# Expert tiles of routed batches written between the transforms of later batches, with transforms of 39 by 64

## The chip, the cores and the metric

The kernel runs on one core of a Trainium2 chip. Its time is the device time of one execution in microseconds (us), the median of several; a profile of one execution shows every instruction of the engines: TensorE (PE, with its weight loads as PEld), VectorE (DVE), ScalarE (ACT), GpSimd (POOL) and SyncE (SP, which here issues transfers). Everything is computed in f32.

## The reference

Eight sequences of 2496 tokens with 256 channels are filtered in the frequency domain; then each token goes to the one of eight experts with the largest logit.

```
X = rfft(x, axis=1); Y = X * (filt_r + 1j * filt_i); y = irfft(Y, n=2496)    # x: 8, 2496, 256
t = y.reshape(19968, 256)
logits = t @ w_gate;  e = argmax(logits);  p = exp(logits - max) / (sum + 1e-9) at e
out = p * (relu(t @ w1[e]) @ w2[e])            # w1: 8, 256, 1024; w2: 8, 1024, 256
```

## The kernel before

A sequence of 2496 is split in 96 and 26, and its transform runs in four products with tables of sines and cosines. A (`stage_a`, L251 on) transforms over the 96 in 26 columns, two to a product of 512 columns, and stores z to DRAM. B and C (`stage_bc`) load z the other way round: B transforms over the 26 for one frequency class a product (256 columns), VectorE multiplies two classes by the filter in one operation of 104 x 1024 (L275), and C transforms back (L282, L286) and stores u. D (`stage_d`) loads u, transforms back over the 96 (L301), stores the tokens to `yd` in DRAM, turns them (L307) and takes the logits (L315). A strip is four columns or four classes, one load and one store each.

`route` finds each token's expert on VectorE, counts tokens per expert with two small products (L351, L352), and GpSimd scatters each token's number and gate into a table in DRAM that is sorted by expert, one indirect transfer a column (L373, 26 a batch).

The batches run in rounds: B and C of batch b, A of batch b + 1 and D of batch b - 1 are handed out strip by strip in turn (`run_all`). A scheduler orders the instructions of this part on each engine. When all eight are routed, `tile_map` makes a list of expert tiles on VectorE: 31 tiles of 512 rows, 8 of 256 and 23 of 128, each of one expert. All of w2 (8 MB) is loaded then and stays on the chip; w1 of a tile's expert (1 MB) is loaded tile by tile.

The expert part is in the order it is written in. For a tile: `gather` loads its part of the table and gathers its rows, 128 at a time, on GpSimd's queue (L490); `turn_x` turns them on PE (L506); `hidden` makes eight products over the 256 channels with relu (L517, halves of 128); `result` sums over the 1024 hidden values for each 128 rows (L531), scales by the gate and scatters the rows to the output on GpSimd's queue (L537). PE's order is hidden of tile i, turn of tile i + 1, result of tile i - 1.

In the profile, each f32 product stands as two records on PE (L531 x2608 are 1304 products), a turn as one.

Of the kernel before, what the change touches and what calls it, by code (L numbers as in the profile page):

```python
# [25 lines left out]
N1 = 96  # L26
N2 = 26
G = N2 // 2
NP = N1 // 4
K2 = 4 * N2  # L30
# [4 lines left out]
def dft_tables():  # L35

    q = np.arange(N1)
    t = np.arange(N2)
    g = np.arange(G)
    w = 2.0 * np.pi

    ta = np.zeros((N1, 2, 2, NP))
    td = np.zeros((2, 2, NP, N2, N1))
    n = N2 * q[None, :] + t[:, None]
    for s in range(2 * NP):  # L50
        h, p = divmod(s, NP)
        if s == 0:
            ta[:, h, 0, p] = 1.0
            ta[:, h, 1, p] = (-1.0) ** q
            td[h, 0, p] = 1.0
            td[h, 1, p] = (-1.0) ** q[None, :]
        else:
            ang = w * ((q * s) % N1) / N1
            ta[:, h, 0, p] = np.cos(ang)
            ta[:, h, 1, p] = -np.sin(ang)  # L60
            ang = w * ((n * s) % S) / S
            td[h, 0, p] = np.cos(ang)
            td[h, 1, p] = -np.sin(ang)
    td *= 2.0 / S


    tb = np.zeros((N2, 2, 2, NP, 2, 2, 2, G))
    for s in range(2 * NP):
        h, p = divmod(s, NP)
        for u in range(2):  # L70
            k = ((N1 - s if s else N1 // 2) if u else s) + N1 * g
            ang = w * ((t[:, None] * k[None, :]) % S) / S
            c, sn = np.cos(ang), np.sin(ang)
            if s == 0:
                tb[:, h, u, p, 0, h, u] = c
                tb[:, h, u, p, 1, h, u] = -sn
            else:
                i = -1.0 if u else 1.0
                tb[:, h, 0, p, 0, h, u] = c
                tb[:, h, 1, p, 0, h, u] = i * sn  # L80
                tb[:, h, 0, p, 1, h, u] = -sn
                tb[:, h, 1, p, 1, h, u] = i * c
    tb[:, 0, :, 0, 1, 0, 0, 0] = 0.0
    tb[:, 0, 0, 0, 1, 0, 0, 0] = (-1.0) ** t


    y = np.zeros((2, 2, 2, 2, G, N2, 2, 2))
    for z in range(2):
        for h in range(2):
            for u in range(2):  # L90
                if z and h == 0:
                    k = (N1 // 2 if u else 0) + N1 * g
                    ang = w * ((k[:, None] * t[None, :]) % S) / S
                    y[z, 0, h, u, :, :, h, u] = np.cos(ang)
                    y[z, 1, h, u, :, :, h, u] = -np.sin(ang)
                    if u == 0:
                        y[z, 0, h, u, 0, :, h, u] = 0.5
                        y[z, 1, h, u, 0, :, h, u] = 0.5 * (-1.0) ** t
                else:
                    ang = w * (((g[:, None] + u) * t[None, :]) % N2) / N2  # L100
                    i = -1.0 if u else 1.0
                    y[z, 0, h, u, :, :, h, 0] = np.cos(ang)
                    y[z, 1, h, u, :, :, h, 0] = -np.sin(ang)
                    y[z, 0, h, u, :, :, h, 1] = i * np.sin(ang)
                    y[z, 1, h, u, :, :, h, 1] = i * np.cos(ang)

    yq = np.stack([y[:, 1], -y[:, 0]], axis=1)
    yq[1, :, 0, 0, 0] = 0.0
    tc = np.stack([y, yq], axis=1).reshape(4, K2, K2).transpose(1, 0, 2)

    return {
        "ta": ta.reshape(N1, N1),
        "tb": tb.reshape(K2, NP, K2),
        "tc": tc,
        "td": td.reshape(N1, N2, N1),
    }
# [3 lines left out]
def kernel(  # L120
# [3 lines left out]
    filt_r: bass.AP,  # L124
    filt_i: bass.AP,
# [6 lines left out]
    td: bass.AP,  # L132
    out: bass.AP,
# [3 lines left out]
    B = x.shape[0]  # L137
    N = B * S

    TILES, left = [], N  # L140
    for rows in (512, 256):
        n = (left - E * (rows - 1)) // rows
        TILES.append((rows, n))
        left -= rows * n
    TILES.append((P, (left + E * (P - 1)) // P))
    TR = E * N + (E + 1) * P
    TR = (TR + 4 * P - 1) // (4 * P) * (4 * P)

    dram = ctx.enter_context(tc.tile_pool(name="dram", bufs=1, space=DRAM))
    zd = [dram.tile([N2, 4, NP, D], F32, tag=f"z{b % 2}", name="zd") for b in range(B)]  # L150
    ud = [dram.tile([N2, 4, NP, D], F32, tag=f"u{b % 2}", name="ud") for b in range(B)]
# [6 lines left out]
    cnt = perm.tile([N1, E], F32, name="cnt")  # L158
    em8 = perm.tile([N1, E], F32, name="em8")
    eoff = perm.tile([N1, E], F32, name="eoff")  # L160
# [4 lines left out]
    psb = fft.enter_context(tc.tile_pool(name="psb", bufs=5, space=PSUM))  # L165
    pst = fft.enter_context(tc.tile_pool(name="pst", bufs=2, space=PSUM))
    psr = fft.enter_context(tc.tile_pool(name="psr", bufs=1, space=PSUM))

    tas = cst.tile([N1, N1], F32, name="tas")
    tbs = cst.tile([K2, NP, K2], F32, name="tbs")  # L170
    tcs = cst.tile([K2, 4, K2], F32, name="tcs")
    tds = cst.tile([N1, N2, N1], F32, name="tds")
    ht = cst.tile([K2, 2, NP, D], F32, name="ht")
    wg = cst.tile([P, DH, E], F32, name="wg")
    tri = cst.tile([N1, N1], F32, name="tri")
    ones = cst.tile([N1, N1], F32, name="ones")
    seg = cst.tile([N1, E, N2], F32, name="seg")
    fill = cst.tile([P, 64, 2], I32, name="fill")
    zrow = cst.tile([1, D], F32, name="zrow")
    ids0 = cst.tile([N1, N2], I32, name="ids0")  # L180
    e_i = cst.tile([N1, E], I32, name="e_i")

    def bank():
        return psb.tile([P, 512], F32, tag="bank", name="bank")

    turn = [0]

    def evac(o, i):
        turn[0] += 1
        if turn[0] % 2:  # L190
            nc.scalar.copy(out=o, in_=i)  # L191
        else:
            nc.vector.tensor_copy(o, i)

    xv = x.rearrange("b (q t) d -> b q t d", t=N2)
    CH = [(t0, min(4, N2 - t0)) for t0 in range(0, N2, 4)]
    PH = [(p0, 4) for p0 in range(0, NP, 4)]


    nc.sync.dma_start(out=tas, in_=ta)  # L200

    def load_filters():
        nc.sync.dma_start(out=tbs, in_=tb)
        for s, f in enumerate((filt_r, filt_i)):
            for h in range(2):
                r = 26 * h
                nc.sync.dma_start(
                    out=ht[r:r + G, s],
                    in_=bass.AP(f.tensor, f.offset + NP * h * D, [[N1 * D, G], [D, NP], [1, D]]),
                )  # L210
                p0 = 1 - h
                nc.sync.dma_start(
                    out=ht[r + G:r + 2 * G, s, p0:],
                    in_=bass.AP(f.tensor, f.offset + (N1 - NP * h - p0) * D, [[N1 * D, G], [-D, NP - p0], [1, D]]),
                )
            nc.sync.dma_start(
                out=ht[G:2 * G, s, 0:1],
                in_=bass.AP(f.tensor, f.offset + N1 // 2 * D, [[N1 * D, G], [D, 1], [1, D]]),
            )
            nc.sync.dma_start(out=ht[2 * N2:K2, s], in_=ht[0:2 * N2, s])  # L220
            nc.sync.dma_start(out=ht[2 * N2:2 * N2 + 1, s, 0, :], in_=f[S // 2:S // 2 + 1, :])
        nc.sync.dma_start(out=tcs, in_=tcm)
# [3 lines left out]
    make_identity(nc, ident)  # L226
    nc.gpsimd.memset(ones, 1.0)
    nc.gpsimd.affine_select(
        out=tri, in_=ones, compare_op=ALU.is_gt, fill=0.0, base=0, pattern=[[1, N1]], channel_multiplier=-1
    )  # L230
    nc.gpsimd.memset(seg, 1.0)
    nc.gpsimd.memset(seg[:, :, 0:1], 0.0)
    nc.gpsimd.memset(cnt, 0.0)
    nc.gpsimd.memset(fill[:, :, 0:1], N)
    nc.gpsimd.memset(fill[:, :, 1:2], 0)
    nc.gpsimd.iota(ids0, pattern=[[1, N2]], base=0, channel_multiplier=N2)
    nc.gpsimd.iota(e_i, pattern=[[1, E]], base=0, channel_multiplier=0)
    nc.vector.tensor_scalar(em8, in0=e_i, scalar1=-float(E), scalar2=None, op0=ALU.add)
    nc.vector.tensor_scalar(eoff, in0=e_i, scalar1=float(N), scalar2=None, op0=ALU.mult)

    def fill_table():
# [6 lines left out]
        nc.sync.dma_start(out=yd[N:N + 1, :], in_=zrow)  # L248


    def stage_a(b):  # L251
        for t0, n in CH:
            xt = sb.tile([N1, 4, D], F32, tag="in", name="xt", bufs=7)
            nc.sync.dma_start(out=xt[:, :n], in_=xv[b, :, t0:t0 + n, :])
            zo = sb.tile([N1, 4, D], F32, tag="st", name="zo", bufs=5)
            for j in range(0, n, 2):
# [329 lines left out]
```

## Time and profile before

| | |
|---|---|
| median of 3 runs | 2347.44 us (2342.65 to 2349.18) |
| the profiled execution | 2343.8 us, span 2342.1 us |
| PE busy | 1904.0 us, 81% of the span |
| mean granted clock of TensorE | 0.873 |
| POOL, DVE, ACT busy | 512.7, 465.6, 323.7 us |
| moved by DMA | 248.33 MB, mean 106 GB/s |

The span runs from the first to the last instruction. A granted clock of 1.00 is 2.4 GHz, 0.50 is 1.2 GHz; a mean between them says what part of a stretch stood at which. Busy time of PE is the time in which a product is in the array, so at a low clock the same work is more busy time. A row of the timeline merges like instructions: start, length, engine, line, operation, and in brackets how long the engine had been idle and what ended it.

### The profile page before, as it was taken

To read this page: it belongs to the slowest core of one execution; us is meant where nothing else is said; L and a number is where in the kernel's file an instruction comes from. 1 tells how busy PE (TensorE), PEld (TensorE's weight loads), DVE (VectorE), ACT (ScalarE), POOL (GpSimd) and SP (SyncE) were. 2 spreads that over 40 slices of the span, in tenths; PEclk is the share of its full clock that TensorE was granted. 3 is DMA by queue.
4 is the path that set the end of the run, shared out by engine and by line. 5 is a ranking of instruction groups with operands and counts; after the bars stand their busy time and mean duration, and the time that the engine had idled before them with its cause. 6 is when DMAs were issued, how large, how long until landed. Compare 5 with 4: busy or idle time off the path is not lost. (4 is left out here: it accounts for less than half of the span.)

```text
span 2342.1 us, 22213 instructions
## 1 busy us (share of the span) xinstructions
PE 1904.0 (81%) x7622; PEld 1261.6 (54%) x7622; DVE 465.6 (20%) x862; ACT 323.7 (14%) x652; POOL 512.7 (22%) x552
## 2 busy tenths in 40 slices
PE   0568858585858677574389999999999999999998
PEld 0224434342434334353156666666666666788997
DVE  0122313131223213122011111111111111111221
ACT  0111111120111111110011111111111111111221
POOL 0000120304040301223332222222222222232221
PEclk9888777786769668675689999999999999999999
DMA  7745434444454535131532222222222221223552
GB/s 143 190 132 155 121 106 129 98 144 90 127 118 145 118 97 153 54 106 27 180 137 85 76 75 72 75 72 75 72 75 75 75 76 65 81 95 117 160 177 74
DMA packets 127203, 248.33 MB, mean 106 GB/s; under 512 B 28007, under 2 KB 79923, under 8 KB 126740
## 3 DMA queue, kind: packets, MB, share of 16 engines
q1 hardware_dynamic: 104792, 204.90, 30.7%
q0 software_dynamic: 22304, 42.01, 5.9%
q8 instruction: 66, 1.08, 0.2%
q14 instruction: 41, 0.34, 0.1%
HBM read 161.05 MB, written 84.16 MB: 105 GB/s over the span
## 5 line engine op out<-in xcount | busy, mean ns | idle before, releaser
L517 PE MATMUL hps<-xT,w1t 128*128 128x512 f32 (+2 forms) x1984 | 577.3, 449 | 0.0
L531 PE MATMUL yps<-w2s,hT 128*128 x2608 | 574.0, 379 | 0.0
L531 PEld LDWEIGHTS yps<-w2s,hT 128*128 128x128 f32 x2608 | 490.7, 190 | 64.9 <-issue 0.3
L517 PEld LDWEIGHTS hps<-xT,w1t 128*128 128x128 f32 x1984 | 324.2, 191 | 234.8 <-issue 224.7
L373 POOL DMA_INDIRECT table<-pay,row x208 | 190.4, 915 | 908.5 <-DVE row L370 569.2
L537 POOL DMA_INDIRECT out_dram<-ys,idt x163 | 163.0, 1000 | 796.4 <-DVE ys L535 540.3
L286 PE MATMUL bank<-pq,tcs 104*104 104x512 f32 x352 | 232.9, 797 | 108.4 <-DVE pq L275 104.5
L520 DVE TENSOR_SCALAR hT<-hps 128x512 f32<-128x512 f32 (+2 forms) x248 | 126.2, 509 | 551.9 <-PE hps L517 539.4
L315 PE MATMUL lg<-wg,yt 128*96 128x8 f32 x832 | 97.8, 244 | 128.3 <-ACT yt L191 62.7
L275 DVE TENSOR_TENSOR pq<-bank,ht 104x1024 f32<-104x1024 f32 x96 | 117.5, 1224 | 364.4 <-PE bank L271 295.8
L521 ACT ACTIVATE hT<-hps 128x512 f32<-128x512 f32 (+2 forms) x248 | 111.9, 451 | 489.4 <-PE hps L517 444.9
L286 PEld LDWEIGHTS bank<-pq,tcs 104*104 104x104 f32 x352 | 66.2, 211 | 203.9 <-DVE pq L275 131.7
L490 POOL DMA_INDIRECT xg<-yd,idt x163 | 157.2, 964 | 83.2 <-issue 45.8
L315 PEld LDWEIGHTS lg<-wg,yt 128*96 128x96 f32 x832 | 94.7, 189 | 147.9 <-ACT yt L191 70.7
L258 PE MATMUL bank<-xt,tas 96*96 96x512 f32 x208 | 119.2, 705 | 65.5 <-DMA xt<-in_x_dram 65.5
L271 PE MATMUL bank<-zi,tbs 104*104 104x256 f32 x384 | 134.6, 476 | 18.1 <-DMA zi<-zd 18.1
L287 ACT COPY uo<-bank 104x512 f32<-104x512 f32 x96 | 56.3, 586 | 575.4 <-PE bank L286 453.2
L271 PEld LDWEIGHTS bank<-zi,tbs 104*104 104x104 f32 x384 | 79.6, 220 | 73.8 <-issue 56.8
L258 PEld LDWEIGHTS bank<-xt,tas 96*96 96x96 f32 x208 | 40.3, 197 | 135.5 <-issue 65.9
L535 DVE TENSOR_SCALAR ys<-yps,idt 128x256 f32<-128x256 f32 x82 | 39.6, 483 | 364.3 <-PE yps L531 364.3
L301 PE MATMUL bank<-ui,tds 96*96 96x256 f32 x416 | 110.3, 404 | 2.0 <-DMA ui<-ud 2.0
L536 ACT ACTIVATE ys<-yps,idt 128x256 f32<-128x256 f32 x81 | 38.4, 474 | 486.6 <-PE yps L531 486.6
(83 smaller groups left out, 648.1 us busy)
## 6 DMA issues: line engine op xcount, KB each, us to landing
w1t<-in_moe_w_dram SPq DMA_DIRECT2D x62, 1024.0 KB
zi<-zd SPq DMA_DIRECT2D x48, 416.0 KB
ud<-uo SPq DMA_DIRECT2D x48, 416.0 KB
xt<-in_x_dram SPq DMA_DIRECT2D x48, 384.0 KB
zd<-zo SPq DMA_DIRECT2D x48, 384.0 KB
ui<-ud SPq DMA_DIRECT2D x48, 384.0 KB
yd<-yo SPq DMA_DIRECT2D x48, 384.0 KB
w2s<-in_moe_w_dram SPq DMA_DIRECT2D x8, 1024.0 KB
```

What stands on the lines that cost most here:

```text
L258: mm(ps[:N1, :], lhsT=tas, rhs=xt[:, j:j + 2, :], start=True, stop=True)
L271: mm(ps[:K2, i * D:(i + 1) * D], lhsT=tbs[:, p0 + j + i, :], rhs=zi[:, j + i, :], start=True, stop=True)
L275: nc.vector.tensor_mul(pq, z2[:, None].to_broadcast((K2, 2, 2, D)), ht[:, :, p0 + j:p0 + j + 2, :])
L286: mm(ps[:K2, :], lhsT=tcs[:, s, :], rhs=pq[:, s], start=(s == 0), stop=(s == 1))
L315: mm(lg[:, 0, t * E:(t + 1) * E], lhsT=yt[:, 2 * i + dh, :], rhs=wg[:, dh, :], start=(dh == 0), stop=(dh == DH - 1))
L373: sc = nc.gpsimd.indirect_dma_start(out=table, out_offset=bass.IndirectOffsetOnAxis(ap=row[:, t:t + 1], axis=0), in_=pay[:, t, :], in_offs ...
L490: nc.gpsimd.indirect_dma_start(out=xgs[i][:, j], out_offset=None, in_=yd, in_offset=bass.IndirectOffsetOnAxis(ap=idt[i].bitcast(U32)[:, j, ...
L517: mm(ps[:, :m], lhsT=w1[:, dh, k * P:(k + 1) * P], rhs=xT[:, dh, :m], start=(dh == 0), stop=(dh == DH - 1))
L520: either(lambda: nc.vector.tensor_scalar_max(hT[:, :m], ps[:, :m], 0.0), lambda: nc.scalar.activation(hT[:, :m], ps[:, :m], AF.Relu))
L521: lambda: nc.scalar.activation(hT[:, :m], ps[:, :m], AF.Relu))
L531: mm(ps, lhsT=hT[k][:, j * P:(j + 1) * P], rhs=w2s[:, bass.ds(ev, 1), k, :], start=(k == 0), stop=(k == FT - 1))
L537: nc.gpsimd.indirect_dma_start(out=out, out_offset=bass.IndirectOffsetOnAxis(ap=ids.bitcast(U32)[:, j, 0:1], axis=0), in_=ys, in_offset=No ...
```

## The change

The sequence is split in 39 and 64. Since three blocks of 39 fill 117 rows, one matrix carries three columns at once: columns 0 to 21, 22 to 42 and 43 to 63 stand in three blocks of partitions (`T0`, `NB`), so there are 22 columns of 117 rows instead of 26 of 96. The 39 real values of a column are 20 frequency classes, so B and C have 20 classes instead of 24, with 128 rows (two halves of 64, real and imaginary) instead of 104. x and the filters are laid out on the host in the order in which they are loaded.

The filter multiply is three multiplies of 512 columns on VectorE and an add on GpSimd for each pair of classes. z and u are stored and loaded in three pieces (one for each block of 39) or two (for each half of 64).

Tiles are made batch by batch: `GROUPS` gives for each batch how many tiles of 512 rows are sure to be full by then (0, 1, 5, 5, 5, 5, 5, 5; the 8 of 256 and 23 of 128 follow the last). w2 is loaded tile by tile as w1 is, two buffers each, and all of it only for the tiles of 128 rows. `transform` and `experts` are two lists of steps with a planned cost each, and one loop writes them out: a tile's step goes next when its inputs should have landed by the planned clock and the credit isn't used up, else a transform step; a transform step gives 2.7 times its cost as credit. PE, VectorE, ScalarE and SP run in the order thus written; GpSimd's order is left to the scheduler. D of a batch is written behind C of the same batch, and A of the next batch between B and C; C of a strip follows B of the next. Copies out of PSUM go to VectorE or ScalarE by planned load, and all stages share seven banks of PSUM.

```diff
-N1 = 96
-N2 = 26
+N1 = 39
+N2 = 64
+NF = (N1 + 1) // 2
+T0 = (0, 22, 43)
+NB = len(T0)
+NG = 22
+TP = NB * N1
...
+    for b in range(B):
+        n = max(0, ((b + 1) * S - (N - left) - E * 511) // 512)
+        GROUPS.append([(512, n)])
+        left -= 512 * n
...
+    def stage_b(b, c):
...
+            for i in range(2):
+                k = HP if f + i == 0 else P
+                mm(p[:, i * D:(i + 1) * D], lhsT=tbs[:k, f + i, :], rhs=zi[:k, j + i, :], start=True, stop=True)
...
+            nc.vector.tensor_mul(yv, z2, ht[:, 0, f:f + 2, :])
+            nc.vector.tensor_mul(yw[:HP], z2[HP:], ht[:HP, 1, f:f + 2, :])
+            nc.vector.tensor_mul(yw[HP:], z2[:HP], ht[HP:, 1, f:f + 2, :])
+            free["v"] = max(free["v"], now[0]) + 2.1
+            ys = outs["y", b, f] = sb.tile([P, 2, D], F32, tag="ysum", name="ysum", bufs=3)
+            nc.gpsimd.tensor_tensor(ys, yv, yw, op=ALU.add)
...
+    def weights(i, second):
...
+        if second:
+            w2t[i] = moe.tile([P, FT, D], F32, tag="w2t", name="w2t")
+            nc.sync.dma_start(out=w2t[i], in_=moe_w2[bass.ds(ev, 1)].rearrange("o p i d -> p (o i) d"))
...
+    def transform():
...
+        for b in range(B):
+            for i in range(nb + 1):
+                if i < nb:
+                    yield lambda: stage_b(b, i), 1.7, None
+                if b + 1 < B:
+                    yield lambda: stage_a(b + 1, i), 0.43 * CH[i][1], ("a", b + 1) if i == nch - 1 else None
+                if 1 <= i:
+                    yield lambda: stage_c(b, i - 1), 1.7, ("c", b) if i == nb else None
+            for i in range(nch + 2):
+                if i < nch:
+                    yield lambda: stage_d(b, i), 0.43 * CH[i][1], None
+                if 2 <= i:
+                    yield lambda: logits(b, i - 2), 0.35 * CH[i - 2][1], None
+                if 1 <= i <= nch:
+                    yield lambda: turn_y(b, i - 1), 0.2 * CH[i - 1][1], None
+            yield lambda: sides.append(after(b)), 0.0, None
...
+    SHARE = 2.7
...
+        while f or e:
+            asked = e and e[2] in when
+            if e and asked and (not f and not sides or when[e[2]] <= now[0] and (credit > 0.0 or not f)):
+                e[0]()
+                now[0] += e[1]
+                credit -= e[1]
+                e = next(es, None)
+            elif f:
+                f[0]()
+                now[0] += f[1]
+                credit = (credit if asked else 0.0) + SHARE * f[1]
...
+            more_loads()
+            side()
...
+            prefetch()
```

`side` writes out one small step of a routed batch's `route` and `tile_map` on VectorE after each step of the loop; `more_loads` keeps up to six strips loaded ahead; `prefetch` asks for a tile's table part, rows and weights up to two tiles ahead.

How the order moves, by two places. On PE before, a step of a round in the middle of the transforms holds C (L286), A (L258), D (L301), turns (L307), logits (L315) and B (L271) of three batches, and no tile:

```order
L286 MATMUL bank<-pq,tcs 104x512 x2
L258 MATMUL bank<-xt,tas 96x512 x2
L301 MATMUL bank<-ui,tds 96x256 x4
L307 MATMUL pt<-ident,yo 128x96 x4
L271 MATMUL bank<-zi,tbs 104x256
L307 MATMUL pt<-ident,yo 128x96 x4
L315 MATMUL lg<-wg,yt 96x8 x4
L271 MATMUL bank<-zi,tbs 104x256
L315 MATMUL lg<-wg,yt 96x8 x4
```

On PE in the change, in batch 4 from C of its fourth strip (L355; lines of the changed kernel) to the first steps of D (L375), with A of batch 5 (L318) and a tile's hidden (L608), turn (L601) and result (L623):

```order
L355 MATMUL bank<-ysum,tcs 128x512 x2
L608 MATMUL bank<-xT,w1t 128x512 x6
L318 MATMUL bank<-fin,tas 117x512
L608 MATMUL bank<-xT,w1t 128x512 x2
L355 MATMUL bank<-ysum,tcs 128x512 x2
L608 MATMUL bank<-xT,w1t 128x512 x6
L375 MATMUL bank<-fin,tds 117x256 x4
L608 MATMUL bank<-xT,w1t 128x512 x2
L601 MATMUL bank<-ident,xg 128x128 x8
L623 MATMUL bank<-w2t,hT 128x256 x8
L375 MATMUL bank<-fin,tds 117x256 x4
```

Two to eight products of a tile now stand between the transform's steps, and six products of 512 columns between the last C and the first D of the batch.

On POOL's queue before, all scatters into the table stand ahead of all gathers (L490) and result stores (L537); here its rows where the experts begin:

```order
L490 DMA xg<-yd,idt 128x256 x20
L537 DMA out_dram<-ys,idt 19968x256 x4
L490 DMA xg<-yd,idt 128x256 x4
L537 DMA out_dram<-ys,idt 19968x256 x4
L490 DMA xg<-yd,idt 128x256 x4
```

On POOL's queue in the change, around the scatters of batch 5 (L476) while batch 6 is transformed, with the adds of the filter multiply (L341), gathers (L574) and result stores (L628):

```order
L341 TENSOR_TENSOR ysum<-yv,yw 128x512
L628 DMA out_dram<-ys,idt 19968x256
L341 TENSOR_TENSOR ysum<-yv,yw 128x512
L628 DMA out_dram<-ys,idt 19968x256 x2
L341 TENSOR_TENSOR ysum<-yv,yw 128x512 x2
L476 DMA table<-pay,row 160896x2 x6
L341 TENSOR_TENSOR ysum<-yv,yw 128x512
L476 DMA table<-pay,row 160896x2 x14
L341 TENSOR_TENSOR ysum<-yv,yw 128x512
L476 DMA table<-pay,row 160896x2 x2
L574 DMA xg<-yd,idt 128x256 x4
```

Adds for C now stand between scatters, gathers and result stores on one queue.

## Rows read from the trace of the kernel before

**Rows 1.** Stretches: length, busy and (records) of each engine, clock, DMA share, GB/s

```profile
core 0: us, PE busy (x) PEld busy (x) DVE busy (x) ACT busy (x) POOL busy (x), PEclk, DMA share, GB/s
69.00:1095.00 1026.00, 727.02 (x2694) 407.49 (x2694) 254.12 (x384) 145.10 (x258) 166.35 (x182) 0.75 0.44 119
1095.00:1168.00 73.00, 19.92 (x47) 9.56 (x48) 17.24 (x85) 2.75 (x5) 28.27 (x33) 0.58 0.41 129
1168.00:2330.00 1162.00, 1150.47 (x4868) 841.37 (x4867) 192.43 (x386) 173.93 (x387) 314.42 (x320) 0.99 0.28 92
```

**Rows 2.** Timeline of PE at the start (start us, us, engine, what)

```profile
5.29 3.70 PE L258 MATMUL bank<-xt,tas 96*96 96x512 f32 x4 [5.29 <-DMA xt<-in_x_dram]
...
69.25 12.28 PE L258 MATMUL bank<-xt,tas 96*96 96x512 f32 x22 [60.25 <-DMA xt<-in_x_dram]
```

**Rows 3.** Timeline of PE, the first expert tile's turn

```profile
1147.73 0.45 PE L506 MATMUL pt<-ident,xg 128*128 128x128 f32 x1 [47.99 <-DMA xg<-yd,idt]
```

**Rows 4.** Timeline of PE, two tiles of 512 rows one after another

```profile
1213.59 13.90 PE L517 MATMUL hps<-xT,w1t 128*128 128x512 f32 x32
...
1242.01 13.90 PE L517 MATMUL hps<-xT,w1t 128*128 128x512 f32 x32
```

**Rows 5.** Timeline of PE, a tile of 256 rows, and PE's end

```profile
2058.56 7.07 PE L517 MATMUL hps<-xT,w1t 128*128 128x256 f32 x32
...
2325.73 7.17 PE L531 MATMUL yps<-w2s,hT 128*128 x32
```

**Rows 6.** Timeline of PE, transforms of batches 0 and 1 at full clock

```profile
101.73 1.88 PE L258 MATMUL bank<-xt,tas 96*96 96x512 f32 x4
103.45 1.03 PE L271 MATMUL bank<-zi,tbs 104*104 104x256 f32 x4
105.80 1.96 PE L286 MATMUL bank<-pq,tcs 104*104 104x512 f32 x4 [1.32 <-DVE pq L275]
...
111.74 1.88 PE L258 MATMUL bank<-xt,tas 96*96 96x512 f32 x4
...
195.67 1.89 PE L301 MATMUL bank<-ui,tds 96*96 96x256 f32 x8
197.42 0.55 PE L307 MATMUL pt<-ident,yo 96*128 96x96 f32 x4
...
198.62 0.83 PE L315 MATMUL lg<-wg,yt 128*96 128x8 f32 x8
199.31 0.66 PE L271 MATMUL bank<-zi,tbs 104*104 104x256 f32 x2
```

**Rows 7.** Stretches: the one with the fastest transfers

```profile
1140.00:1200.00 60.00, 38.13 (x90) 17.59 (x91) 7.32 (x11) 5.95 (x10) 19.00 (x20) 0.75 0.82 272
```

**Rows 8.** Costliest groups by shape: busy, mean ns, idle before and releasers

```profile
L275 DVE TENSOR_TENSOR pq<-bank,ht 104x1024 f32<-104x1024 f32 x96 | 117.5, 1224 | 364.4 <-PE bank L271 295.8 <-remote 60.6 <-issue 8.1
...
L193 DVE COPY zo<-bank 96x512 f32<-96x512 f32 x52 | 35.7, 686 | 252.2 <-PE bank L258 249.3 <-issue 2.9
...
masks.py:199 POOL TENSOR_SCALAR_AFFINE_SELECT ident<-ident 128x128 f32<-128x128 f32 x1 | 0.3, 283 | 0.0
...
L490 POOL DMA_INDIRECT xg<-yd,idt x163 | 157.2, 964 | 83.2 <-issue 45.8 <-DMA idt<-table 26.1 <-DMA out_dram<-ys,idt 8.8
```

**Rows 9.** Timeline of PE, start of B in batch 1

```profile
163.79 2.01 PE L271 MATMUL bank<-zi,tbs 104*104 104x256 f32 x4 [9.27 <-DMA zi<-zd]
...
174.03 3.71 PE L286 MATMUL bank<-pq,tcs 104*104 104x512 f32 x4 [1.41 <-DVE pq L275]
```

**Rows 10.** Timeline of PE, two strips of the last D

```profile
1080.17 2.00 PE L301 MATMUL bank<-ui,tds 96*96 96x256 f32 x4
...
1087.42 2.00 PE L301 MATMUL bank<-ui,tds 96*96 96x256 f32 x4
```

**Rows 11.** Timeline of SP, loads of x

```profile
65.49 2.68 SPq L254 DMA_DIRECT2D xt<-in_x_dram  x6
```

**Rows 12.** Timeline of POOL, scatters into the table

```profile
1104.42 0.92 POOL L373 DMA_INDIRECT table<-pay,row  x1 [0.30 <-issue]
```

More of the change, by code (lines that the diff above doesn't have):

```diff
@@ L235 @@
[L235 to L241, printed above, removed]
+        nc.sync.dma_start(out=ids0, in_=ids)
+        nc.sync.dma_start(out=vld, in_=valid)
         rows = table.rearrange("(p i) c -> p i c", p=P)
@@ L546 @@
-    n = len(work)
-    with tc.manual_schedule():
-        for i in range(-3, n + 1):
-            if 0 <= i + 3 < n:
-                gather(i + 3)
-                weights(i + 3)
-                if i + 3 == 0:
-                    for e in range(E):
-                        nc.sync.dma_start(out=w2s[:, e], in_=moe_w2[e].rearrange("(i p) d -> p i d", p=P))
-            if i == -1:
-                turn_x(0)
-            if 0 <= i < n:
-                hidden(i)
-            if 0 <= i and i + 1 < n:
-                turn_x(i + 1)
-            if 1 <= i:
-                result(i - 1)
@@ new lines, in after, with side, prefetch, may @@
+    def after(b):
+        yield from route(b)
+        for rows, n in GROUPS[b]:
+            if n:
+                yield from tile_map(b, rows, n, rows == P)
+    def side():
+        while sides:
+            try:
+                return next(sides[0])
+            except StopIteration:
+                sides.pop(0)
+    got = {"list": 0, "x": 0, "w1": 0, "w2": 0}
+    used = {"x": 0, "w1": 0, "w2": 0}
+    when = {}
+    GAP = {"list": 5.0, "x": 7.0, "w1": 9.0, "w2": 9.0}
+    def prefetch():
+        def may(what, depth):
+            i = got[what]
+            deep = depth if i < SHORT else 4
+            return i < len(work) and i - used.get(what, used["w1"]) < deep
+        def mark(what):
+            when[what, got[what]] = now[0] + GAP[what]
+            got[what] += 1
+        if may("list", 3):
+            listed(got["list"])
+            mark("list")
+        i = got["x"]
+        if i < got["list"] and i - used["x"] < 2 and when["list", i] <= now[0]:
+            gather(i)
+            mark("x")
+        for what in ("w1", "w2"):
+            if got[what] < got["list"] and may(what, 2):
+                weights(got[what], what == "w2")
+                mark(what)
@@ new lines, in experts @@
+    def experts():
+        for i in range(NT):
+            n = TILES[i][0]
+            if used["x"] == i:
+                yield lambda: turn_x(i), 0.22 * n, ("x", i)
+                used["x"] += 1
+            for k in range(FT):
+                yield lambda: hidden(i, k), 0.43 * n, ("w1", i)
+            w1t.pop(i), xts.pop(i)
+            used["w1"] += 1
+            if i + 1 < NT and when.get(("x", i + 1), now[0] + 1.0) <= now[0]:
+                yield lambda: turn_x(i + 1), 0.22 * TILES[i + 1][0], ("x", i + 1)
+                used["x"] += 1
+            for j in range(n):
+                yield lambda: result(i, j), 3.42, ("w2", i)
+            hs.pop(i), idt.pop(i), w2t.pop(i, None)
+            used["w2"] += 1
```

747 lines of the change are left out of this document (424 added, 323 removed).

## The prediction

> **What bounds the kernel now.** I read the table of stretches first, then PE's timeline, then the costliest groups, then the transfers. The table [rows 1] splits the span in four. Up to 69 us almost nothing is computed: one strip of x is transformed at 5.29 and the next only at 69.25, after PE had waited 60.25 us for x behind the filter loads [rows 2]. From 69 to 1095 the eight transforms run: PE is busy 727 of 1026 us and its granted clock is 0.75 on average, so nearly half of the stretch stands at the lower level of 1.2 GHz. From 1095 to 1168 only the last routing is left: PE waits 47.99 us for the first gathered rows [rows 3]. From 1168 to the end the experts run with PE busy 1150 of 1162 us at 0.99. So the end is set by a stage of about 1170 us in which only TensorE counts, and ahead of it stand 1150 us in which TensorE idles or is slow. What the change can win is the second part; the first it can only keep or spoil.
>
> **PE's work, in durations at 2.4 GHz.** An expert tile of 512 rows takes 28.42 us, from one start of its first product to the next [rows 4]. The 8 tiles of 256 and 23 of 128 rows take 281.4 us: from 2058.56 to 2325.73 + 7.17, and 7.07 for the first product of the first, which lies before [rows 5]. Both counts stay as they are (31, 8, 23). In the transforms two 512-column products take 103.45 - 101.73 = 1.72 us, four of 256 columns 197.42 - 195.67 = 1.75 (eight records), four turns 0.55, four logit products 199.31 - 198.62 = 0.69 [rows 6]. Per batch the kernel before has 35 products of 512 columns (13 at A, 22 at C), 54 of 256 (24, 4, 26), 52 turns and 52 logit products: 30.1 + 23.6 + 7.2 + 9.0 = 69.9 us. The changed one has 20, 44, 44 and 44: 17.2 + 19.3 + 6.1 + 7.6 = 50.2 us, of which D with its turns and logits are 23.3. Eight batches are 559 us before, over 1026: the transforms run at 0.55 of what PE could do. That share, not the work, is the point of the change.
>
> **The change part by part.** The changed order has four sections; I price them in turn.
>
> *Batch 0* has no cover. It must bring x (2.9 MB), the five filter strips with their tables (6.6), the rest of the tables and the table's fill (2.5), and store and load z, store u and transform batch 1's x beside it: some 24 MB before C is done. The fastest stretch of the trace moved 272 GB/s at a share of 0.82 [rows 7], which gives 88 us; at the 119 GB/s of the transform stretch it would be 200. The filters are now whole-partition copies in strips, so I stay near the first: 100 us, and 40 more for D. Batch 0 ends at 140 (110 to 170). The wait of 60 us for x goes, since all six strips of x now stand on SP's queue ahead of the filters.
>
> *Batches 1 and 2* run as transforms alone. B, A and C of a strip are 1.75 + 1.72 + 1.72 = 5.2 us of PE; the same three cost the kernel before 111.74 - 101.73 = 10.0 us at the full clock, since each pair of products waited 1.32 us for VectorE's filter multiply [rows 6]. C is now written one strip later, so that wait has a strip's time to pass. In its place stands a longer chain: three multiplies of 512 columns instead of one of 1024, then an add on GpSimd. A multiply of 512 lies between half of 1224 ns and the 686 ns of a 512-column copy [rows 8]; at 0.65 us, six are 3.9 us a strip, below 5.2. The add isn't in this trace; by the copy and by four times the 283 ns of a 128-column GpSimd operation it takes 0.69 to 1.13 us [rows 8], two a strip, also covered. The Trainium skill (GPSIMD Engine Reference, 3.1 Elementwise) advises against such an add and gives 4497 ns at 2048 elements, an estimate of 1.1 us here; by it the sum stays the same. Transfers are what is late next: x, z twice and u are 2 MB a strip, 7.4 us at 272 GB/s. I take 8 us a strip and 45 for the five with their lag. Then D waits for u to go out and come back; the like trip of z cost 9.27 us [rows 9]. D ran alone at the end of the transforms before, one strip in 1087.42 - 1080.17 = 7.25 us at the low clock [rows 10], 40 us for 5.5 strips; at the full clock it is 23.3, and I take 32. Sum 45 + 9 + 32 = 86, with 2 for the routing's PE work: 88 a batch. Bounds: 5 x 5.2 + 5 + 9 + 23 = 63 below, and above it the kernel before's own pace: from B of batch 1 at 163.79 [rows 9] to 1095 stand eight rounds, 116 each. SP issues 80 transfers a batch instead of 40; at the 0.45 us apiece at which it issued x [rows 11] that is 36 us, covered.
>
> *Batch 3 up to its D* holds the only tile that batches 0 and 1 can fill: 45 + 28.4 + 9, and 7 for the tile's gather, which stands on GpSimd's queue behind the adds of batch 3: 89 (70 to 130). So tiles flow from 140 + 2 x 88 + 89 = 405 us on; bounds 306 and 532.
>
> *From there on* PE has 30 tiles (852.6), the short ones (281.4), D of batch 3 and four batches (23.3 + 200.8 = 224). The transforms' waits are hidden behind tiles where the order places some between: 3 to 6 us of tile work at each turn from C to D, against 9.27 needed, so 3 to 6 us stay open at each of four turns. GpSimd's queue is strictly in the order shown: a batch's 22 scatters take 1.22 us each [rows 12], 27 us, and C's adds stand between and behind them. Per batch it holds 27 + 40 gathers and result stores of about 1.26 (50) + adds (11) = 88 us, against 50.2 + 5 x 28.4 = 192 of PE: no bound, but an add can be late by part of a burst; 5 us each time. Weights are loaded a tile ahead (42 us of lead); with them a batch moves 31 MB in 192 us, 161 GB/s, under the 272 seen. With each open wait PE's clock may fall: after the 9.27 us wait the products ran at half pace (3.71 us instead of 1.96 for four) [rows 6, 9]. I put all this at 50 us; below it could be 0, as in the expert stage now, above it is the third rival's.
>
> *The end* stays: 9.2 us from PE's last product (2332.9) to the end of the span.
>
> Sum: 405 + 852.6 + 281.4 + 224 + 50 + 9.2 = 1822 us of span, against 2342.1. The profiled execution lies 1.7 us above its span and 3.6 below the median of the runs, so I forecast 1827.
>
> **The rivals.** First, the lead-in keeps its old pace: 532 instead of 405 us, in all 1954. For it speak the clock of 0.75 and twice as many transfers; against it the removed 1.32 us waits. Second, all goes as the order means it: lead-in 340, stalls 10, in all 1722; for it speaks that PE never idled in the expert stage. Third, tiles and transforms together get the transforms' clock. That part is 224 + 20 tiles (568) = 792 us of PE work; at a mean of 0.75 it takes 1056, in all 2041 with the 50 as part of it. This is also what a rule makes of it. The Trainium skill (TensorE: Matmul & The Clock Gate, "A second HAM failure mode: psum-queue depth-cycling") has the clock oscillate where PE idles briefly while PSUM banks are cycled, and here all stages share seven banks. The trace bears this out for the transforms and not for the experts, whose seven banks cycled at 0.99. Fourth, GpSimd's queue: if PE waits out the whole burst of 27 us in each of four batches, 108 more, in all 1935. Fifth, on the other side: the joint part runs at the transforms' 0.55 of PE's pace, with idle time and low clock together, because each strip's chain (VectorE, GpSimd, a DRAM trip) holds up the tile products behind it on PE's single queue. 792 / 0.55 = 1440, or 648 more: 2425 without the 50, slower than before. It decides from 792 / (792 + 570) = 0.58 of full pace downwards. For it speaks that PE takes its queue in order; against it that the order puts 2 to 14 us of tile work between the steps of a chain. That the order isn't what the words say is no rival: tiles do stand between strips.
>
> **Chances.** Forecast 0.60 (own range 1750 to 1890), lead-in 0.13, all smooth 0.12, clock 0.05, GpSimd 0.06, slower 0.04. The range runs from 1730 to 1950: it leaves out the clock, the slower case, about half of the smooth one and a third of the lead-in. A change of 0.3%, some 7 us, is what can be told from none; only cases on the far side can lie within it: faster 0.95, same 0.01, slower 0.04.
>
> **What would show it.** In the changed profile the first tile's turn should stand near 350 us and tiles flow from about 405; batches 1 and 2 should take 80 to 95 us each from B to B, with a wait of about 9 us before each D; from 405 on PE should be busy over 90% at a clock above 0.95; D's wait for u should show in the joint part as 3 to 6 us each; GpSimd's adds should take about 1 us. I am wrong if PE waits for the adds or the multiplies by more than some 2 us a strip, if the clock in the joint part is below 0.9, if gathers or weights end PE's waits there, or if the lead-in lies outside 306 to 532.

## The result, and the profile after

The changed kernel takes 1914.75 us (median of 4 runs, 1913.90 to 1920.21) against 2347.15 for the kernel before beside it: a ratio of 0.8165 (95% interval 0.8146 to 0.8184), faster. The forecast was 1827 with a range of 1730 to 1950, so the time lies in the range and 88 us above the forecast. The profiled execution took 1913.90 us, its span 1912.2.

The stretches of the changed kernel answer to [rows 1]: batch 0, batch 1, batch 2, batch 3 up to its first strip of D, tiles and transforms together, and tiles alone. The columns are those of [rows 1].

```profile
0.00:129.70 129.70, 77.81 (x282) 47.86 (x282) 35.98 (x59) 22.67 (x39) 14.61 (x28) 0.79 0.85 258
129.70:232.90 103.20, 67.36 (x266) 44.46 (x265) 35.71 (x64) 18.11 (x33) 34.42 (x32) 0.71 0.56 153
232.90:337.70 104.80, 68.38 (x266) 45.16 (x264) 38.38 (x86) 18.10 (x33) 34.26 (x32) 0.71 0.57 156
337.70:441.70 104.00, 67.31 (x194) 39.49 (x193) 35.41 (x79) 17.11 (x30) 46.12 (x45) 0.81 0.44 130
441.70:1385.00 943.30, 877.83 (x3466) 593.89 (x3467) 244.03 (x534) 176.54 (x315) 334.96 (x333) 0.95 0.49 141
1385.00:1912.20 527.20, 517.01 (x2564) 417.54 (x2562) 132.87 (x391) 50.51 (x102) 133.23 (x135) 0.99 0.44 153
```

Batch 0 runs near the fastest transfers of [rows 7] (258 against 272 GB/s) and ends at 129.7. Batches 1 and 2 take 103 and 105 us, though PE is busy for 67 and 68. From 442 on the clock is near full, but PE is idle for 65 of 943 us. The timeline of PE in batch 1 shows where the time of the transforms goes; it answers to [rows 6, 9].

```profile
147.29 1.89 PE L331 MATMUL bank<-fin,tbs 128*128 128x256 f32 x8
149.02 1.88 PE L318 MATMUL bank<-fin,tas 117*117 117x512 f32 x4
150.74 1.88 PE L355 MATMUL bank<-ysum,tcs 128*128 128x512 f32 x4
152.46 1.89 PE L331 MATMUL bank<-fin,tbs 128*128 128x256 f32 x8
...
162.26 1.02 PE L355 MATMUL bank<-ysum,tcs 128*128 128x512 f32 x2
177.94 2.08 PE L355 MATMUL bank<-ysum,tcs 128*128 128x512 f32 x2 [14.66 <-POOL ysum L341]
180.12 2.03 PE L318 MATMUL bank<-fin,tas 117*117 117x512 f32 x2
186.87 2.07 PE L355 MATMUL bank<-ysum,tcs 128*128 128x512 f32 x2 [4.72 <-POOL ysum L341]
191.84 2.07 PE L355 MATMUL bank<-ysum,tcs 128*128 128x512 f32 x2 [2.89 <-POOL ysum L341]
203.32 3.31 PE L375 MATMUL bank<-fin,tds 117*117 117x256 f32 x7 [9.41 <-DMA fin<-ud]
```

A strip of B, A and C runs without a gap in 152.46 - 147.29 = 5.17 us at first. Then C waits three times for GpSimd's add, 14.66 + 4.72 + 2.89 = 22.3 us, and runs at half pace behind the first (2.08 us instead of 1.02 for two records). The queue of POOL at the same time says why; the scatters are those of [rows 12].

```profile
159.99 1.15 POOL L476 DMA_INDIRECT table<-pay,row  x1 [1.27 <-DMA zd<-zo]
...
175.61 0.98 POOL L476 DMA_INDIRECT table<-pay,row  x1 [0.30 <-issue]
176.63 1.26 POOL L341 TENSOR_TENSOR ysum<-yv,yw 128x512 f32<-128x512 f32 x1
178.08 1.00 POOL L476 DMA_INDIRECT table<-pay,row  x1 [0.19 <-issue]
...
185.54 1.27 POOL L341 TENSOR_TENSOR ysum<-yv,yw 128x512 f32<-128x512 f32 x1
```

Thirteen scatters of batch 0 stand ahead of one add of batch 1, six ahead of the next, three ahead of a third, 1.29 us each with the gap. The waits of PE from 441 to 1400 (engine, line, waited for: us in total, times, longest) show the other part.

```profile
PE bank L375 <- DMA fin<-ud: 35.8, 5, 18.3
PE bank L623 <- issue: 18.7, 20, 2.9
PE bank L355 <- POOL ysum L341: 7.0, 2, 5.7
PE bank L355 <- DVE yw L338: 6.0, 1, 6.0
```

The longest wait of the first line, 18.3 us, ends with the first D of batch 3 at 441.7, so it still belongs to the lead-in; 17.5 us are left for the joint part. The second line is a wait for nothing that the profile names. 12.9 of its 18.7 us fall into the longest run of GpSimd's transfers, batch 7's 22 scatters (1322.6 to 1350.6) and the four gathers behind them, as the timeline of PE shows; the gaps begin some 20 us into that run:

```profile
1334.10 8.58 PE L623 MATMUL bank<-w2t,hT 128*128 128x256 f32 x39
1344.01 0.81 PE L623 MATMUL bank<-w2t,hT 128*128 128x256 f32 x3 [1.33 <-issue]
1346.84 0.38 PE L623 MATMUL bank<-w2t,hT 128*128 128x256 f32 x1 [2.02 <-issue]
...
1353.20 0.58 PE L623 MATMUL bank<-w2t,hT 128*128 128x256 f32 x1 [2.92 <-issue]
...
1359.52 3.06 PE L623 MATMUL bank<-w2t,hT 128*128 128x256 f32 x5 [0.84 <-issue]
```

For some 17 us PE executes one or a few records at a time with gaps of up to 2.9 us, and the granted clock is 0.50 from 1351 to 1361, the lower level (up to 0.59 us a record against 0.22).

### The profile page after: what moved, and what is told of

Same layout as the page of the kernel before. It is cut to its first block, busy times and chain, and to the rows that moved or that the text cites. A ratio compares the mean times of both kernels' runs of the same rounds, so it can differ in the third digit from the quotient of the medians.

```text
span 1912.2 us, 21011 instructions
## 1 busy us (share of the span) xinstructions
PE 1675.7 (88%) x7030; PEld 1188.4 (62%) x7030; DVE 522.4 (27%) x1211; ACT 303.0 (16%) x552; POOL 597.6 (31%) x605
## 5 line engine op out<-in xcount | busy, mean ns | idle before, releaser
L608 PE MATMUL bank<-xT,w1t 128*128 128x512 f32 (+2 forms) x1984 | 593.6, 453 | 0.6 <-ACT xT L229 0.6
L623 PE MATMUL bank<-w2t,hT 128*128 128x256 f32 x2240 | 515.6, 386 | 24.9 <-issue 24.7
L623 PEld LDWEIGHTS bank<-w2t,hT 128*128 128x128 f32 x2240 | 428.6, 193 | 97.9 <-issue 41.2
L608 PEld LDWEIGHTS bank<-xT,w1t 128*128 128x128 f32 x1984 | 324.1, 193 | 223.2 <-issue 205.9
L628 POOL DMA_INDIRECT out_dram<-ys,idt x163 | 163.1, 1001 | 649.5 <-DVE ys L626 337.7
L574 POOL DMA_INDIRECT xg<-yd,idt x163 | 157.4, 966 | 290.5 <-PE bank L601 222.2
L612 ACT ACTIVATE hT<-bank 128x512 f32<-128x512 f32 x248 | 147.9, 597 | 541.2 <-PE bank L608 497.3
L341 POOL TENSOR_TENSOR ysum<-yv,yw 128x512 f32<-128x512 f32 x80 | 101.9, 1274 | 298.6 <-DVE yw L338 279.2
L476 POOL DMA_INDIRECT table<-pay,row x176 | 172.9, 982 | 66.2 <-issue 51.1
L355 PE MATMUL bank<-ysum,tcs 128*128 128x512 f32 x144 | 90.4, 737 | 80.6 <-POOL ysum L341 56.4
L375 PE MATMUL bank<-fin,tds 117*117 117x256 f32 (+1 forms) x352 | 100.8, 435 | 64.1 <-DMA fin<-ud 64.1
L375 PEld LDWEIGHTS bank<-fin,tds 117*117 117x117 f32 (+1 forms) x352 | 69.9, 208 | 92.0 <-issue 74.4
L331 PE MATMUL bank<-fin,tbs 128*128 128x256 f32 (+1 forms) x320 | 91.9, 431 | 19.5 <-DMA fin<-zd 15.7
L355 PEld LDWEIGHTS bank<-ysum,tcs 128*128 128x128 f32 x144 | 30.1, 225 | 121.9 <-POOL ysum L341 73.2
L318 PE MATMUL bank<-fin,tas 117*117 117x512 f32 x176 | 91.4, 645 | 6.4 <-DMA fin<-in_x_dram 5.3
L623 PE MATMUL bank<-w2s,hT 128*128 x368 | 83.2, 379 | 0.0
```

Source lines behind the costliest of these rows:

```text
L318: mm(p[:TP, :], lhsT=tas, rhs=xt[:TP, j:j + 2, :], start=True, stop=True)
L331: mm(p[:, i * D:(i + 1) * D], lhsT=tbs[:k, f + i, :], rhs=zi[:k, j + i, :], start=True, stop=True)
L341: nc.gpsimd.tensor_tensor(ys, yv, yw, op=ALU.add)
L355: mm(p, lhsT=tcs[:, 1, :], rhs=ys, start=True, stop=True)
L375: mm(p[:k, i * D:(i + 1) * D], lhsT=tds[:k, i0 + j + i, :k], rhs=ui[:k, j + i, :], start=True, stop=True)
L476: sc = nc.gpsimd.indirect_dma_start(out=table, out_offset=bass.IndirectOffsetOnAxis(ap=row[:k, t:t + 1], axis=0), in_=pay[:k, t, :], in_of ...
```

## The experiments

Every trace was split at the first record of D in batch 3: the lead-in before it, and the rest. e1 to e4 and e9 to e12 ran on one chip, e5 to e8 on another. e2, e5, e8 and e10 start with a table filled in advance and write no routed rows to it, so they compute something else and only price the scatters. Of each edit the main lines are shown, "..." marks what is left out.

| run | median us | ratio to before beside it | lead-in | rest |
|---|---|---|---|---|
| changed kernel | 1914.75 | 0.8165 (0.8146 to 0.8184) | 441.7 | 1470.5 |
| e9, the same again | 1913.47 | 0.8156 (0.8114 to 0.8198) | 448.9 | 1470.0 |
| e1, add on VectorE | 1913.12 | 0.8136 (0.8081 to 0.8190) | 420.2 | 1488.0 |
| e2, no scatters | 1779.12 | 0.7565 (0.7515 to 0.7615) | 373.5 | 1400.9 |
| e3, scatters spread | 1871.11 | 0.7956 (0.7901 to 0.8012) | 399.0 | 1471.6 |
| e5, empty scatters | 1872.96 | 0.8658 (0.8583 to 0.8734) | 440.9 | 1430.8 |
| e6, e3 with e1 | 1826.57 | 0.8447 (0.8374 to 0.8519) | 391.9 | 1430.1 |
| e7, e6 with hold | 1796.24 | 0.8301 (0.8228 to 0.8373) | 395.0 | 1403.8 |
| e10, e5 with e1 | 1902.44 | 0.8101 (0.8055 to 0.8148) | 423.6 | 1476.5 |
| e11, hold alone | 1880.97 | 0.8032 (0.7987 to 0.8076) | 436.2 | 1439.8 |
| e12, e7 and later rk | 1783.18 | 0.7596 (0.7553 to 0.7639) | 389.3 | 1398.0 |

**e1, the add on VectorE.**

```diff
-            nc.gpsimd.tensor_tensor(ys, yv, yw, op=ALU.add)
+            nc.vector.tensor_tensor(ys, yv, yw, op=ALU.add)
...
```

> The add of each pair of strips stands on VectorE instead of GpSimd (with five instead of three ysum buffers, and one instead of two for each of its two operands); GpSimd's scatters stay. Theory A: the changed kernel lost most of its 88 us over the forecast to the adds that stand behind a batch's 22 scatters on GpSimd (22 us of PE's waits for ysum in each of batches 1 and 2, 7 to 13 later) and to slow spells of PE during the bursts. Then PE's waits for ysum in C go, batches 1 and 2 take about 84 us each instead of 104, the slow spells stay, and the time is 1865 us (1850 to 1880). Theory B: the loss is the trip of u through DRAM between C and D and the clock that falls with it; then 1905 or more. Theory C: the add's own 1.27 us on GpSimd is what is slow; it foresees the same as A here, and is told apart by the run without scatters.

1913.12 us: A and C missed, and B has the number without the reason. The lead-in won 21.5 us, the rest lost 17.5. The waits for POOL's ysum are gone, but without adds between them all 22 scatters of a batch run as one piece (169.9 to 198.1 in batch 1), and now beside the trip of u. SP's 18 loads of u take 17.03 us to issue, and PE waits 14.00 instead of 9.41 before D:

```profile
184.60 17.03 SPq L310 DMA_DIRECT2D fin<-ud  x18
191.55 6.00 PE L375 MATMUL bank<-fin,tds 117*117 117x256 f32 x16 [14.00 <-issue]
```

In the rest PE's waits on issue rise from 26.1 to 37.0 us, and two waits for ScalarE of 10.2 and 11.3 us are new; what these two hang on stays open.

**e2, no scatters.**

```diff
...
-            sc = nc.gpsimd.indirect_dma_start(
-                out=table,
...
```

> The 22 scatters of each batch are left out; the table is filled at the start with row numbers 0 to 2047 in turn and gates of 1 instead, so that gathers and result stores move as many bytes as before, of other rows. Everything else, the adds on GpSimd too, stays. Theory A: both parts of the loss go, the waits for ysum (44 us in batches 1 and 2, some 10 later) and the slow spells (some 30 us): 1830 us (1815 to 1845), with batches 1 and 2 at about 83 us and no stretch in which PE executes single products 1.5 to 2.9 us apart. Theory B (DRAM trip and clock): no less than 1895. Theory C (the add itself is slow): batches 1 and 2 still take over 100 us, 1880 or more in all.

1779.12 us, 136 less than the changed kernel and 36 below theory A's lower end: A named the cause and undersized it. B and C fall. Batch 1 and the same loads as above:

```profile
131.54:206.22 74.68, 58.25 (x265) 40.86 (x264) 35.74 (x64) 18.03 (x33) 12.71 (x10) 0.87 0.74 214
```

```profile
173.80 10.54 SPq L309 DMA_DIRECT2D fin<-ud  x18
```

The batch takes 74.7 us instead of 103.2, of which 22.3 are the waits for ysum and 9.1 PE's work at a higher clock (58.3 instead of 67.4 us busy at 0.87 instead of 0.71); its other waits are 3 us longer. The loads go out in 10.54 us. No wait of PE on issue is left. From the first D of batch 3 on, the changed kernel and e2 compare so:

```profile
441.70:1912.20 1470.50, 1394.84 (x6028) 1011.43 (x6028) 376.90 (x923) 227.04 (x417) 468.19 (x468) 0.97 0.47 145
```

```profile
373.50:1774.40 1400.90, 1369.79 (x6028) 1003.06 (x6028) 375.89 (x923) 227.65 (x417) 361.32 (x358) 0.99 0.47 153
```

Of the 69.6 us that the scatters cost there, 44.5 are idle time of PE and 25.1 the same records taking longer.

**e3, scatters spread.**

```diff
-        nc.vector.tensor_copy(row, rowf)
...
+            if t % 2 == 0:
+                nc.vector.tensor_copy(row[:, t:t + 2], rowf[:, t:t + 2])
...
-            if t % 2:
-                yield
+            yield
```

> The 22 columns of row numbers are converted in 11 pieces of two, one piece every second step of VectorE's hand-written order, instead of in one; so a batch's scatters become ready two by two, and GpSimd's queue holds them between adds, gathers and stores instead of in one piece of 22. Nothing is left out. Theory A: waits for ysum shrink from 22 to 3 to 6 us a batch in batches 1 and 2, and the slow spells of PE go where scatters no longer follow each other without a gap: 1850 us (1835 to 1870). If it is the number of scatters and not their density that slows the other engines, the spells are only thinned out and the time is 1870 to 1885. Theory B: 1905 or more, and slower still if a later listing holds tiles back.

1871.11 us, just past theory A's upper end and into the reading by number. The lead-in won 43; the rest won nothing, although the slow spells went (PE's waits on issue are 3.8 us in the whole trace), so it isn't the number that stayed: adds now wait behind single scatters, gathers and stores (41.8 us of PE's waits for ysum in 12).

**e4, tiles apart.**

```diff
...
-    SHARE = 2.7
+    SHARE = 0.0
```

> No expert tile is placed before the last transform (SHARE 0; the small rows of the tile map get eight buffers, and the results three instead of four); the new split with its tables and whole-partition loads stays. It prices the two halves of the change apart. If the seven later batches all go at the 104 us of batches 1 and 2, the transforms end near 130 + 7 x 104 = 858, the last routing and first gather take some 50, and 31 tiles of 28.42, the short ones and the end 1172: 2080 us (2050 to 2110), so the split is worth about 270 us and the interleaving 165. If instead the interleaving carries most of the gain, 2250 or more; if it carries nearly none, under 1980.

2029.25 us (ratio 0.8627, 0.8569 to 0.8685), below the expected 2050 to 2110: B of batches 1 to 7 starts 102.6 us apart as expected, but the last batch has no A beside it and the first tile, listed long before, turns at 836 instead of some 910. The split and its tables are worth 2347 - 2029 = 318 us, the interleaving 2029 - 1915 = 114.

**e5, empty scatters, and e10, empty scatters with the add on VectorE.**

```diff
...
-        nc.vector.tensor_copy(row, rowf)
+        nc.vector.tensor_scalar(row, in0=rowf, scalar1=1.0, scalar2=None, op0=ALU.add)
...
                 in_=pay[:k, t, :],
...
+                bounds_check=0,
+                oob_is_err=False,
```

> The 22 scatters of each batch stay on GpSimd's queue, but every row number lies past their bound (row + 1 against a bound of 0), so that they write nothing; the table is filled at the start with row numbers 0 to 2047 and gates of 1, as in the run without scatters. It tells apart what in a scatter costs the 136 us that its absence gave back (1915 to 1779). Theory W, the 117 writes of 8 bytes to DRAM hold up the other transfers, loads of instructions among them: then only the adds' place behind the instructions on GpSimd is left, 22 us in each of batches 1 and 2 and some 10 to 20 later, 1840 us (1825 to 1860). Theory G, GpSimd's own work of making the transfers is what slows the others: 1895 or more. If the empty ones take GpSimd far less than 1.29 us each, both parts go and the time is near 1785; then only the price of an instruction was found.

> The scatters write nothing, as in e5, and the add stands on VectorE, as in e1. Each alone gave little (1873 and 1913 against 1915), the absence of scatters gave 136. If the loss is two things, the adds' place behind the scatters and the hold that the writes put on other work, and each hides the other where they fall into the same stretch, both edits together give nearly all of it: 1785 us (1770 to 1800). If GpSimd's instructions hold up the other engines or the transfers even where they write nothing, 1820 or more.

An empty scatter takes GpSimd 987 ns on average, a writing one 982. e5's 1872.96 lies between both theories and on another chip than e9, the changed kernel again. Its lead-in won nothing, as it would if the place on the queue alone counts there. e10 settles the writes: on e1's chip and with its scatters emptied, it takes 1902.44 against 1913.12, so the writes of 8 bytes cost some 11 us, and the expected 1785 of two additive parts falls. Beside the trip of u it is the writes that count: with 22 empty scatters in one piece there, SP's 18 loads go out in 10.55 us in batch 1 and 10.83 in batch 2, against 17.03 and 17.64 in e1, and PE waits 9.20 and 9.65 before D, against 14.00 and 13.07. The batches get hardly shorter by it, since PE then waits longer for other inputs (batch 1 takes 92.1 us against 92.5). The slow spells need no writes, as PE's timeline of e10 shows:

```profile
1324.76 9.66 PE L624 MATMUL bank<-w2t,hT 128*128 128x256 f32 x44
1335.76 0.38 PE L624 MATMUL bank<-w2t,hT 128*128 128x256 f32 x1 [1.33 <-issue]
...
1349.05 5.32 PE L624 MATMUL bank<-w2t,hT 128*128 128x256 f32 x13 [1.50 <-issue]
```

In sum there are 38.5 us of such waits in the second products of e10. On the other chip e5 has 1.4 us of waits on issue in all, though its longest runs, of 22 scatters in one piece, hold no add either: beside the last of them (from 1300.5) the 64 records of second products take 13.98 us without a gap. So the adds between are not the difference there. All experiments with such spells ran on the first chip, which makes the chip the likeliest cause, but no run repeats the changed kernel or one of these on both.

**e6, spread, and the add on VectorE** (the edits of e3 and e1).

> Both edits together: the row numbers become ready two by two at every second step, and the add stands on VectorE (with the buffers of the first run). Alone, the spreading left 41.8 us of PE's waits for ysum and 8.3 for yw in the trace of 1870.5, and the add on VectorE left the bursts. Theory A (adds behind the scatters, and density of the scatters): the waits for ysum go, and the time is 1832 us (1815 to 1850). Theory V, VectorE becomes late in place of GpSimd, since it takes 80 adds of 0.69 us: 1860 or more. Theory N, it is the number of scatters that costs, whatever stands between them: what is left above the 1779 without scatters stays near 90, 1865 or more.

1826.57 us, as theory A has it. V and N fall. The two edits win 44 and 2 apart, 88 together, on another chip, though.

**e7 and e11, expert work between C and D.**

```diff
+    HOLD, hold = 10.0, 0.0
...
-            if e and asked and (not f and not sides or when[e[2]] <= now[0] and (credit > 0.0 or not f)):
+            if e and asked and (not f and not sides or when[e[2]] <= now[0] and (credit > 0.0 or not f or now[0] < hold)):
...
                 stored.add(f[2])
+                if f[2] and f[2][0] == "c":
+                    hold = now[0] + HOLD
```

> As the run before, and after the last strip of C of a batch the order places expert work, where there is any, until 10 us of it stand before the first strip of D, whatever the share is by then. The trace of the changed kernel has 35.8 us of PE's waits for u in the joint part, five of them. Theory B's part of the loss: these waits shrink to some 5 us, and PE's clock stays up behind them: 20 us less than the run before (10 to 30). Rival: the expert work placed there is missing later, or the trip takes as much longer as it gets cover: within 6 us of the run before.

> The changed kernel with one edit: after the last strip of C, expert work is placed until 10 us of it stand before D. Of the 35.8 us of waits for u in the joint part the first, 18.3, lies where there is no tile to place, the other four are 17.5. If those are what the trip costs, 1895 us (1885 to 1905); if the order behind it only shifts, within 6 us of the changed kernel; by e7, which took 30 us less than e6, 1885.

e7 took 30 us less than e6, the upper end of what was expected, and the hold alone 1880.97 against e9's 1913.47 on the same chip, below the 1885 to 1905 that the waits themselves would give. From the first D of batch 3 on, e9 and e11 compare so:

```profile
448.90:1919.00 1470.10, 1389.43 (x6028) 1007.51 (x6028) 380.38 (x923) 226.90 (x417) 469.32 (x468) 0.97 0.47 145
```

```profile
436.20:1876.00 1439.80, 1379.96 (x6028) 1004.00 (x6028) 376.08 (x923) 226.85 (x417) 468.39 (x468) 0.97 0.48 148
```

The 30.2 us are 20.8 less idle time of PE and 9.5 us less for the same records. The waits for u behind the first D fall from 16.5 to 0.5 us, all other waits together by 4.8. PE runs at half pace behind such waits, as in batch 1 above, so an idle time saved brings more than its length.

**e8, the kernel before without scatters.**

> The kernel before with its 26 scatters of each batch left out, and the table filled at the start with row numbers 0 to 2047 and gates of 1. It asks whether the price was there before the change. If a batch's scatters cost the kernel before as much as the changed one (136 us in all), 2210 us, and the forecast's rows held it unseen; if its slower transforms hid them, 2310 or more, and the change brought the price out; between, 2240 to 2290, partly.

On that chip the kernel before takes 2171.15 us itself, so the expected times can't be compared, only the difference: 2132.24, ratio 0.9864 (0.9779 to 0.9950), some 30 us by the ratio, too near to none for a clear verdict. So there the kernel before pays far less for its scatters than the 136 us of the changed one on the first chip. Why is not shown: its transforms are slower, and it has no adds on GpSimd's queue that could wait behind them.

**e9, the changed kernel again, and e12, the routing's products two steps later.**

```diff
...
+        yield
+        yield
         rk = psr.tile([TP, 2, E * NG], F32, tag="lg", name="rk")
```

> The changed kernel itself, beside the next three and on the same chip. In the run beside e5 to e8 the kernel before took 2171 us, and 2349 beside e1 to e4 (granted clock about 0.905 against 0.873). If the changed kernel too depends on the chip so, the experiments of the two groups can't be set against each other as they stand; if it doesn't, it takes 1915 us (1900 to 1925) here again, and only the kernel before moves.

> As e7 (row numbers in pieces of two, add on VectorE, 10 us of expert work between C and D), and the routing's two small products stand two steps later in PE's order, where e7's trace has 24.7 us of waits for oe in six of them. These waits shrink to under 8 us, and the time is 1782 us (1770 to 1795) against e7's 1796; if the scatters, now later by two steps, come to lie beside D and its trip, 1796 or more.

e9 repeats the changed kernel's time on e1's chip; on the other one it wasn't run. e12 takes 1783.18 us, as expected, and is the fastest version that computes everything: 130 us less than e9 beside it. Its waits from 395 to 1250 answer to the table of the changed kernel:

```profile
PE bank L375 <- DMA fin<-ud: 6.4, 6, 3.4
PE bank L603 <- DMA xg<-yd,idt: 3.9, 2, 3.4
PE rk L445 <- DVE oe L434: 2.5, 1, 2.5
```

Its rest of 1398.0 us is that of e2 without any scatter (1400.9), which has neither the hold nor the later products, though. It was gained on the first chip with e7's edits and one more, which had 24.7 us of waits to win; so most of e6's and e7's gains can't be the other chip's.

## Why the prediction was right, and where it was off

The time lies in the range of 1730 to 1950, but above the 1750 to 1890 that the forecast gave itself: the room left for the rivals took it in. One sign of being wrong came true. PE waited for the adds by 22.3 us over five strips in batch 1, about 4.5 a strip, where 2 was the bound. The mechanism of the gain stood as forecast: transforms without the old waits, and tiles between them at nearly full clock (PE busy for 93% at 0.95). What the scatters do to it was missing from the forecast.

**Lead-in, 405 forecast, 441.7 measured.** Batch 0 ended at 129.7 (forecast 140). The full-clock strip of B, A and C took the forecast 5.2 us, and the wait of 1.32 us per pair [rows 6] went. The step that failed is the sum of 88 us for batches 1 and 2, and of 89 for batch 3: 103.2, 104.8 and 104.0. It was made of two errors. The transforms themselves were priced too high: without scatters they take 74.7. And the previous batch's 22 scatters were not in it at all; the text put them into the joint part only. They cost 28.5 and 30.3 us in batches 1 and 2 and 11.2 in batch 3 (e2), as waits for adds queued behind them and by the lower clock. That the first error hid 13 us a batch of the second is luck. Batch 3 has a third error, in the trip of u below.

**Joint part and end, 1417 forecast, 1470.5 measured.** The tiles kept their 28.42 us [rows 4], as these two starts of second products behind each other show:

```profile
1381.03 13.82 PE bank L623 x64
1409.45 13.82 PE bank L623 x64
```

The work without any stall is 1367 by the forecast's terms, and without scatters this part takes 1400.9, so the work was priced well, and the mis-sized term is the stalls: 50 forecast, 103 measured, of which 34 remain without scatters. "5 us each time" for an add behind part of a burst was near the truth (1.3 to 5.7). What was missing is the slow spells beside a dense run of GpSimd's instructions, on engines that don't wait for it, and the slower products behind each idle time (25.1 of the 69.6 us). How the 69.6 us divide between spells and late adds isn't shown: with the spells gone and more late adds, e3 has the same rest.

**The trip of u.** Forecast 9 us in batches 1 and 2 and 3 to 6 at four turns; measured 9.41 in both, then 4.48, 6.72, 3.47 and 2.85, and 18.26 in batch 3, where 9 was forecast. No tile covers it, as in batches 1 and 2, but here the loads for the next tile stand ahead of the last store of u on SP's queue:

```profile
424.17 0.37 SPq L558 DMA_DIRECT2D idt<-table  x1
425.34 0.37 SPq L593 DMA_DIRECT2D w1t<-in_moe_w_dram  x1
426.50 0.34 SPq L589 DMA_DIRECT2D w2t<-in_moe_w_dram  x1
426.95 0.46 SPq L357 DMA_DIRECT2D ud<-uo  x1
427.46 0.61 SPq L358 DMA_DIRECT2D ud<-uo  x1
436.94 10.23 SPq L310 DMA_DIRECT2D fin<-ud  x18
```

The load of u starts 8.9 us after its last store was issued, against 2.8 in batch 1. e2 has the same order and waits 18.36 there; e3 and e12, with no weights issued between, wait 12.22 and 13.20. No run changed this order alone.

**GpSimd's add.** Bounded by 0.69 and 1.13 us, measured 1274 ns (the multiply 689, forecast 0.65):

```profile
L341 POOL TENSOR_TENSOR ysum<-yv,yw 128x512 f32<-128x512 f32 x80 | 101.9, 1274 | 298.6 <-DVE yw L338 279.2 <-PE bank L353 12.9 <-PE bank L355 6.0
```

The estimate of 1.1 us from the Trainium skill (GPSIMD Engine Reference, 3.1 Elementwise) lies by the upper row, and both are low. The add's speed didn't matter; its place on the queue did, as e2 and e3 show in the lead-in, where the same adds on the same engine wait less.

**The rivals.** The fourth had the mechanism, a burst that PE waits out, at 1935 and with 0.06; it hit in two lead-in batches and not in the four joint ones. The first fell, with a lead-in of 441.7 and not 532. The third and the fifth fell: the joint part ran at 0.95 of the clock. The second, all smooth at 1722, needs a lead-in of 340; without scatters it is 373.5.

## What to carry to other kernels

List for each in-order queue everything that one stage leaves on it for the next, not only in the part where the stages are interleaved: here one batch's bookkeeping stood ahead of the next batch's arithmetic on GpSimd. When such a queue is cleared by moving the arithmetic away, what stays on it becomes denser and can hold up others, so spread it by when its inputs become ready. Price an idle time of PE above its length, since the products behind it run slower: in batch 1 (e2) 19.4 us of idle time came with 9.1 us of slower products, in the joint part 44.5 with 25.1 (e2) and 20.8 with 9.5 (e11), about a half on top each time.

## What the runs showed of the hardware that was not expected

- Some 20 us into a dense run of GpSimd's indirect transfers PE slowed to single records with no releaser in the profile, even where the transfers write nothing (e10). It was seen on one of the two chips only, and mostly beside the second products of tiles; beside the runs of 22 in e10's batches 1 and 2, with no tile, PE waited 0.9 and 1.9 us on issue. Spread so that at most 18 (e3) or 16 (e12) follow each other, 3.8 and 0.4 us of such waits were left in the whole trace. What holds PE was not found.
- Scatters that write lengthened the issue of SP's loads beside them: 18 loads took 17.03 us beside 22 that write (e1) and 10.55 beside 22 that write nothing (e10).
- The kernel before takes 2344 to 2349 us on one chip and 2171 on another (2146 to 2180, granted clock 0.902 to 0.917 instead of 0.867 to 0.880 over these runs), with the same program. Whether the changed one moves so was not tried.
